# Attention and routed experts on one core: the first routing round's comparisons, counts and pick cut in halves and 128 columns wide, fewer warming products, and a new order of the experts' work

## The chip, the cores and the metric

The kernel runs on one core of a Trainium2 chip. The metric is the device time of one execution, in microseconds (us); lower is better. TensorE (PE) has two clock levels, 1.2 and 2.4 GHz; the profile lists the granted clock as a share of the higher one. PE does the matrix products, VectorE (DVE) and ScalarE (ACT) the elementwise work, GpSimd (POOL) issues the gathers and scatters of rows by index, SyncE (SP) issues the other transfers.

## The reference

Windowed attention with four sink positions makes a table `x` of 3072 tokens by 512. A gate gives each token a logit for each of 8 experts. The pairs of token and expert are taken in falling order of logit; a token goes to the first expert that still has room (384 places). Each expert runs a two-layer network on its 384 tokens.

```python
logits = x @ w_gate
order = np.argsort(-logits.flatten())
for idx in order:
    tok, e = idx // E, idx % E
    if assigned[tok] >= 0 or counts[e] >= cap: continue
    assigned[tok] = e; counts[e] += 1
for e in range(E):
    mask = assigned == e
    out[mask] = np.maximum(x[mask] @ w1[e], 0.0) @ w2[e]
```

## The kernel before

**Attention** (the first 152 us) works on 24 blocks of 128 tokens and writes `x` to memory and the logits to `L`. Its order is not touched.

**Routing** runs in 8 rounds, one for each expert that fills up (`phase`, L534). A round finds the logit at which the first expert is full by a search over the bits of the logits in six steps (`STEPS`: two steps of 64 candidates, four of 32). One step is a chain between two engines: DVE compares all 24 columns of tokens with the candidates (`compare`, L486, writes `cmp`), PE counts per expert (L557, the comparison is the weight operand, the experts' mask `oh` streams), DVE finds the step's digit (`i`, L574 or L580 to 585), PE spreads it over the partitions (L589 or L590, the "digit product" below), DVE forms the next threshold (`xb`) and compares again. At the end of a round come ranks (L617, L618), a comparison of ranks (`lo` against a row of 64) and a second product, the pick (L636), whose result are the indices `idx` of the expert's tokens. In the first round the counts are 24 products whose weights are 64 or 32 columns wide, and the pick is 24 products of 64 columns; in later rounds several columns are packed to 128, so 12 or 6 products do.

**An expert** (`rows`, `weights`, `mlp`): POOL gathers the token rows into `xg0`, `xg1`, `xg2` (L682); PE turns them (L689) into `pt`, `py0`, `py1`; ACT makes the high part `xh` (L700), DVE the low part `xl` (L702). Weights come in 8 loads of 512 KB into four buffers `raw0` to `raw3` (L673); ACT makes the high part `wh` (L675), DVE the low part `wl` (L677). For the first expert, loads 2 to 7 wait until `xg2` has landed (L663, "rowed"). A tile of the first layer is `ph` (eight tiles, f = 0 to 7); for each of four chunks c it takes three products: `xh` with `wh`, `xh` with `wl`, `xl` with `wh` (L722), 96 products per expert. ACT applies Relu (`hh`), DVE makes the low part `hl`. The second layer sums into `py` (L734, 72 products), ACT copies it to `yo`, POOL scatters it to the output (L739).

**Order.** Every engine runs its own list in order. `Graph.order` makes these lists for the routing and the experts: a list scheduler with estimated costs and delays, in which each task's priority is its longest path to the end plus a number for its class (`BIAS`: R for the routing of a round, X for turning, M for products and so on). `run` (L755) also puts warming products (128x384, results unused, L532) in gaps of PE's list between the first pick and the first expert's products, as many as its estimate of the gap holds (L762). In the first round `WARM` gives each step one or two warming products ahead of its counts, and three ahead of the pick.

## Time and profile before

| | |
|---|---|
| median of 3 runs | 502.12 us (499.77 to 504.07) |
| the profiled execution's own time | 499.03 us |
| its span in the trace | 497.3 us |
| busy share of the span: PE, DVE, ACT, POOL | 95%, 77%, 47%, 30% |
| mean granted clock of PE | 0.976 |

The profiled execution is one run, so rows of its trace add up to 499.03 us: 497.3 us of span and 1.7 us around it. A busy share counts a product from its start to its modelled end, and products overlap; so the spacing of products (time of a chain divided by their number) says more than the mean length of one. Positions below are us from the start of the span.

### The profile page before, as it was taken

The numbers are of one execution on the slowest core, as the hardware profiler recorded it, in microseconds if no ns is written. First come the engines' busy times: TensorE is split into PE (matmuls) and PEld (weight loads), VectorE is DVE, ScalarE is ACT, GpSimd is POOL, SyncE is SP. The second block draws the span as 40 slices with busy tenths as digits, with TensorE's granted clock in tenths as the row PEclk, the third lists the DMA queues.
The fourth block names the chain that finished last, engine by engine and source line by source line (L and its number), as shares of the span: only waits on it lengthen the run. The fifth ranks groups of instructions, "written<-read, shape, count | busy, mean of one in ns | idle before, by whom it ended". The sixth has DMA issues, their size and how long they took to land. (4 is left out here: it accounts for less than half of the span.)

```text
span 497.3 us, 11371 instructions
## 1 busy us (share of the span) xinstructions
PE 470.7 (95%) x4167; PEld 388.5 (78%) x4167; DVE 380.9 (77%) x1141; ACT 233.7 (47%) x672; POOL 148.3 (30%) x210
## 2 busy tenths in 40 slices
PE   8999999999997698999999999998999999999994
PEld 4878788887875466878878978876887888988983
DVE  5699989999997589989898898897899864640200
ACT  4678887787860045344353362353352265531210
POOL 6567575665541020030222110032201251001001
PEclk9999999999997589999999999999999999999998
DMA  8556677766412264472572470571652787401001
GB/s 267 190 168 177 176 193 198 207 174 173 106 46 65 68 201 138 153 198 89 177 238 79 165 244 37 164 233 71 209 156 80 229 265 245 173 0 43 21 22 43
DMA packets 75464, 73.13 MB, mean 147 GB/s; under 512 B 28560, under 2 KB 57872, under 8 KB 75408
## 3 DMA queue, kind: packets, MB, share of 16 engines
q1 hardware_dynamic: 70992, 59.29, 40.3%
q0 software_dynamic: 3840, 12.59, 7.4%
q8 instruction: 33, 0.54, 0.4%
q10 hardware_dynamic: 576, 0.52, 0.4%
q14 instruction: 23, 0.19, 0.1%
HBM read 59.80 MB, written 12.58 MB: 146 GB/s over the span
## 5 line engine op out<-in xcount | busy, mean ns | idle before, releaser
L675 ACT ACTIVATE wh<-raw 128x1024 fp32r<-128x1024 f32 x64 | 67.7, 1061 | 76.9 <-DMA raw<-w 41.4
L722 PE MATMUL ph<-xh,wh 128*128 128x384 f32 x256 | 91.4, 357 | 1.0 <-DVE hl L726 0.7
L677 DVE TENSOR_TENSOR wl<-raw,wh 128x1024 fp32r<-128x1024 f32 x64 | 77.5, 1216 | 18.6 <-ACT wh L675 18.3
L722 PE MATMUL ph<-xl,wh 128*128 128x384 f32 x256 | 86.5, 338 | 0.4 <-DVE xl L712 0.4
L722 PE MATMUL ph<-xh,wl 128*128 128x384 f32 x256 | 86.2, 337 | 0.0
L739 POOL DMA_INDIRECT out<-yo,idx x24 | 26.1, 1088 | 178.3 <-ACT yo L737 132.0
L734 PE MATMUL py<-wh,hh 128*128 128x512 f32 x192 | 78.3, 408 | 0.5 <-ACT yo L737 0.4
L734 PE MATMUL py<-wh,hl 128*128 128x512 f32 x192 | 75.5, 393 | 0.3 <-DVE hl L726 0.2
L734 PE MATMUL py<-wl,hh 128*128 128x512 f32 x192 | 75.3, 392 | 0.0
L96 ACT ACTIVATE P<-pp,nmx 128x132 f32<-128x132 f32 x192 | 68.6, 370 | 8.0 <-DVE nmx L91 6.6
L725 ACT ACTIVATE hh<-ph 128x384 fp32r<-128x384 f32 x64 | 31.1, 487 | 78.4 <-PE ph L722 63.4
L81 PE MATMUL pp<-kk,q 64*128 64x260 f32 (+1 forms) x384 | 60.7, 421 | 2.3 <-ACT P L96 1.0
L726 DVE SCALAR_TENSOR_TENSOR hl<-ph,hh 128x384 fp32r<-128x384 f32 x64 | 34.6, 550 | 31.4 <-ACT hh L725 31.1
L682 POOL DMA_INDIRECT xg<-x_dram,idx x24 | 27.6, 1150 | 102.0 <-PE ph L722 41.4
L722 PEld LDWEIGHTS ph<-xh,wh 128*128 128x128 f32 x256 | 48.2, 188 | 4.7 <-DVE hl L726 2.4
L722 PEld LDWEIGHTS ph<-xh,wl 128*128 128x128 f32 x256 | 48.2, 188 | 1.3
L722 PEld LDWEIGHTS ph<-xl,wh 128*128 128x128 f32 x256 | 48.0, 188 | 1.2 <-DVE xl L712 0.7
L81 PEld LDWEIGHTS pp<-kk,q 64*128 64x128 f32 x384 | 33.7, 208 | 14.4 <-ACT P L96 7.3
L734 PEld LDWEIGHTS py<-wh,hl 128*128 128x128 f32 x192 | 36.0, 188 | 9.1 <-DVE hl L726 1.2
L734 PEld LDWEIGHTS py<-wh,hh 128*128 128x128 f32 x192 | 36.2, 188 | 8.0 <-issue 2.0
L91 DVE TENSOR_REDUCE nmx<-pp 128x2 f32<-128x264 f32 x96 | 39.8, 426 | 1.0
L103 ACT ACTIVATE PT<-pp 128x512 f32<-128x512 f32 x48 | 28.7, 597 | 24.0 <-PE pp L102 19.7
(172 smaller groups left out, 827.7 us busy)
## 6 DMA issues: line engine op xcount, KB each, us to landing
raw<-w SPq DMA_DIRECT2D x64, 512.0 KB, 4.7
v<-vd SPq DMA_DIRECT2D x24, 256.0 KB, 3.6
x_dram<-xt SPq DMA_DIRECT2D x24, 256.0 KB, 3.1
kk<-kd SPq DMA_DIRECT2D x23, 264.0 KB, 4.4
q<-qd SPq DMA_DIRECT2D x22, 256.0 KB, 4.3
xg<-x_dram,idx POOLq DMA_INDIRECT x24, 4.1
out<-yo,idx POOLq DMA_INDIRECT x24, 3.0
us<-ud SPq DMA_DIRECT2D x1, 274.5 KB, 5.7
```

The source lines that it names most:

```text
L81: PE.matmul(sp[:,s,:n],q[p,g,:],kk[p,g,k0:k0+n],start=True,stop=True)
L91: V.tensor_reduce(T('nmx',c)[:,2*g:2*g+2],sp[:,:,o:o+132],AX.X,OP.max,negate=True)
L96: A.activation(T('P',c)[:,4*s+g,:],sp[:,s,o:o+132],AF.Exp,bias=T('nmx',c)[:,h:h+1],scale=1.0,accum_out=T('sm',c)[:,h:h+1])
L103: def op_pe(c,g): A.activation(T('PT',c)[:,4*g:4*g+4,:].rearrange("p j (s n)->p s j n",s=2),T('p',c,f'T{g}')[:,:,0:256].rearrange("p s (j ...
L675: g.add('A',947,lambda wh=wh,raw=raw: nc.scalar.activation(wh,raw,AF.Copy),[f'raw{n%4}'],[f'wh{s}'],f'H{k}.{j}',f'W{k}')
L677: g.add(e,{'V':1135,'P':2303}[e],lambda wh=wh,wl=wl,raw=raw,e=e: (nc.vector if e=='V' else nc.gpsimd).tensor_tensor(wl,raw,wh.bitcast(F32) ...
L682: g.add('P',1450,lambda t=t: nc.gpsimd.indirect_dma_start(out=self.xg[t],out_offset=None,in_=self.x_dram,in_offset=bass.IndirectOffsetOnAx ...
L722: nc.tensor.matmul(p[:,0:CAP],x[:,c,:],y[:,c,:],start=c==0 and i==0,stop=c==3 and i==2)
L725: g.add('A',371,lambda f=f,p=p: nc.scalar.activation(self.hh[:,f,:],p[:,0:CAP],AF.Relu),ps,[f'hh{f}'],f'hh{k}.{f}',f'H{k}')
L726: g.add('V',469,lambda f=f,p=p: nc.vector.scalar_tensor_tensor(self.hl[:,f,:],p[:,0:CAP],0.0,self.hh[:,f,:].bitcast(F32),op0=OP.max,op1=OP ...
L734: nc.tensor.matmul(p,x[:,f,ts],w,start=f==0 and i==0,stop=f==7 and i==2)
L739: st=nc.gpsimd.indirect_dma_start(out=self.out,out_offset=bass.IndirectOffsetOnAxis(ap=idx[:,t:t+1],axis=0),in_=y,in_offset=None)
```

## The change

1. **Halves (first round only).** From the second step on, the comparison is issued as two: 13 of 24 columns, then 11 (64 candidates); 15, then 9 (32 candidates). The counts are issued as two tasks of 12 products, of which the first needs only the first comparison. The comparison of ranks and the pick are cut the same way, and the small operations `hi`, `R`, `R3` on which the pick also rests go ahead of the comparison.
2. **128 columns.** The counts and the pick of the first round read 128 columns of the comparison as weights for each product, where they read 64 or 32; the rows that belong to the next columns are not used. `cmp` gets 64 spare columns, zeroed by two more POOL memsets at the start of the program.
3. **Low parts last.** For the first two tiles of the first expert the four chunks' `xh` products come first, the four `xl` products last (8 tasks instead of 4).
4. **Turning first.** The second round's first counts are held until the first expert's rows are turned.
5. **Fewer warming products** after the first pick: a gap holds (gap - 400)/260 instead of (gap - 170)/165.
6. **Order searched anew:** all of `BIAS` is new, and a table `TW` gives single tasks a number of their own.

```diff
-        pri=[-(rank[i]+bias.get(T[i][5],0.0)) for i in range(n)]
+        pri=[TW.get(i,0)-(rank[i]+bias.get(T[i][5],0.0)) for i in range(n)]
...
-        self.cmp=[t([128,64*NC],BF,f"cmp{j}") for j in range(2)]
+        self.cmp=[t([128,64*NC+64],BF,f"cmp{j}") for j in range(2)]
...
+        for x in self.cmp: g.memset(x[:,64*NC:],0.0)
...
+                if n and first:
+                    hv=NC//2+128//m-1
+                    v(u(hv*m/2),lambda j=j,m=m,hv=hv: self.compare(j,xb[j],m,0,hv),f'xb{j}',cn+'a')
+                    v(u((NC-hv)*m/2),lambda j=j,m=m,hv=hv: self.compare(j,xb[j],m,hv,NC),f'xb{j}',cn)
...
-                    for c in range(h):
-                        nc.tensor.matmul(cnt[0:z*m,0:z*E],self.cmp[j][:,c*z*m:c*z*m+z*m],self.oh[:,z*c:z*c+z],start=c==0 and (end or not first),stop=c==h-1)
+                    for c in range(c0,c1):
+                        nc.tensor.matmul(cnt[:,0:z*E],self.cmp[j][:,c*z*m:c*z*m+128],self.oh[:,z*c:z*c+z],start=c==0 and (end or not first),stop=c==h-1)
...
+        if first:
+            hv=NC//2+1
+            v(u(hv*32),lambda: self.compare(oj,self.lo,64,0,hv,OP.is_equal,F16),'lo R3',on+'a')
+            v(u((NC-hv)*32),lambda: self.compare(oj,self.lo,64,hv,NC,OP.is_equal,F16),'lo',on)
...
+            for c in range(c0,c1): nc.tensor.matmul(ip[:,0:6*zp],OH[:,64*zp*c:64*zp*c+128],self.R3[:,:,zp*c:zp*c+zp].rearrange("p g j -> p j g"),start=c==0,stop=c==h-1)
...
-                    g.add('E',125,lambda t=t,d=d,tp=tp: turn(t,d,tp),[f'xg{t}'],ts,f'X{k}.{d}.{t}',f'X{k}')
+                    g.add('E',125,lambda t=t,d=d,tp=tp: turn(t,d,tp),[f'xg{t}'],ts+['turned'],f'X{k}.{d}.{t}',f'X{k}')
...
+            three=((wh,self.xh[b],'h'),(wl,self.xh[b],'h'),(wh,self.xl[b],'l'))
+            parts=[[(c,i) for i in range(3)] for c in range(4)] if k or f>1 else [[(c,0),(c,1)] for c in range(4)]+[[(c,2)] for c in range(4)]
...
-            if s-te>340 and te>=tr: ex.append((te+1,int((s-te-170)//165)))
+            if s-te>340 and te>=tr: ex.append((te+1,int((s-te-400)//260)))
```

On DVE, after the ranks of the first round (`q` holds ranks, `lo` and `hi` their low and high bits, `cmp0` the comparison, `R3` what the pick streams). Before:

```order
L623 TENSOR_TENSOR si_104<-q_131 128x24
L625 TENSOR_SCALAR lo_109<-si_104 128x48
L489 TENSOR_TENSOR cmp0_114<-lo_109,row_66 128x1536
L624 TENSOR_SCALAR hi_132<-si_104 128x24
L630 TENSOR_TENSOR R_150<-hi_132,g6_133 128x144
L632 TENSOR_TENSOR R3_151<-R_150,tid_88 128x144
```

Now:

```order
L631 TENSOR_TENSOR si_104<-q_131 128x24
L632 TENSOR_SCALAR hi_132<-si_104 128x24
L633 TENSOR_SCALAR lo_109<-si_104 128x48
L638 TENSOR_TENSOR R_152<-hi_132,g6_133 128x144
L639 TENSOR_TENSOR R3_153<-R_152,tid_88 128x144
L490 TENSOR_TENSOR cmp0_114<-lo_109,row_66 128x832
L490 TENSOR_TENSOR cmp0_114<-lo_109,row_66 128x704
```

The three small operations moved from behind the comparison to its front, and the comparison is two.

On PE, from the turning of the first expert's last rows to its first products. Before, with ten warming products and the second round's second counts (12 products) in between:

```order
L689 MATMUL pt_2436<-idt_62,xg2_2426 128x64 x4
L689 MATMUL py0_2439<-idt_62,xg2_2426 128x64
...
L532 MATMUL ph1_2438<-onesb_80 128x384
...
L557 MATMUL pr0_2441<-oh_111,cmp1_115 128x16
...
L722 MATMUL ph0_2437<-xh0_2427,wh0_2400 128x384
L722 MATMUL ph0_2437<-xh0_2427,wl0_2412 128x384
L722 MATMUL ph0_2437<-xl0_2429,wh0_2400 128x384
```

Now, with the second round's first counts (12 products) in between:

```order
L704 MATMUL pt_2438<-idt_62,xg2_2428 128x64 x4
L704 MATMUL py0_2441<-idt_62,xg2_2428 128x64
...
L562 MATMUL pr0_2443<-oh_111,cmp0_114 128x16
...
L738 MATMUL ph1_2440<-xh0_2429,wh0_2402 128x384
L738 MATMUL ph1_2440<-xh0_2429,wl0_2414 128x384
L738 MATMUL ph0_2439<-xh0_2429,wh0_2402 128x384
```

No warming product stands there now, and the first `xl` product comes after 14 products with `xh`. Ahead of it, from the first pick on, there were 23, 5 and 3 warming products around the turns of `xg0`, `xg1`, `xg2`; there are 19 ahead of `xg0`, none ahead of `xg1` and 2 ahead of `xg2`, and the second round's first counts moved behind the turns.

On DVE, the work on the first expert's weights beside the second round's steps (`odd`, `two`, `i81` find the digit, `P0` and `xb` form the threshold). Before:

```order
L677 TENSOR_TENSOR wl1_2413<-raw1_2397,wh1_2401 128x1024
L580 TENSOR_SCALAR odd_120<-pr0_2441 64x16
L581 TENSOR_TENSOR two_121<-pr0_2441,odd_120 64x16
L584 TENSOR_SCALAR odd_120<-two_121 32x8
L585 SCALAR_TENSOR_TENSOR i81_117<-two_121,odd_120 32x8
L677 TENSOR_TENSOR wl2_2414<-raw2_2398,wh2_2402 128x1024
L597 TENSOR_REDUCE P0_123<-pr1_2442 128x1
L600 TENSOR_TENSOR xb1_108<-x0_105,P0_123 128x48
L489 TENSOR_TENSOR cmp1_115<-xb1_108,row_66 128x768
```

Now:

```order
L515 CAST df_113<-di_112 128x120
L692 TENSOR_TENSOR wl1_2415<-raw1_2399,wh1_2403 128x1024
L692 TENSOR_TENSOR wl0_2414<-raw0_2398,wh0_2402 128x1024
...
L593 SCALAR_TENSOR_TENSOR i80_116<-pr0_2443,odd_120 64x8
L692 TENSOR_TENSOR wl2_2416<-raw2_2400,wh2_2404 128x1024
L605 TENSOR_REDUCE P1_124<-pr1_2444 128x1
L608 TENSOR_TENSOR xb0_107<-x1_106,P1_124 128x48
L575 SCALAR_TENSOR_TENSOR x0_105<-P1_124,y_103 128x24
L490 TENSOR_TENSOR cmp0_114<-xb0_107,row_66 128x768
```

`wl1` moved ahead of all of the second round's steps (it stood in the third), and `wl2` moved from the step before the fourth counts (`cmp1`) to the step before the third (`cmp0`). Behind that `cmp0` the two `hl` of the first two tiles follow, as one does in the list of before.

## Rows read from the trace of the kernel before

**Rows 1.** Waits of PE from 183 us on: total, times, longest (first and last of 7).
```profile
PE pr L590 <- DVE i L585: 2.0, 2, 1.8
...
PE py L734 <- DVE hl L726: 0.2, 1, 0.2
```

**Rows 2.** Chain that ended last, in order of time: start, us, what.
```profile
422.29 4.19 PE ph L722 x24
...
488.08 2.72 DMA out<-yo,idx
```

**Rows 3.** Two-us stretches: length, busy us of the engines, PE clock, DMA share, GB/s.
```profile
154.00:156.00 2.00, 0.97 (x26) 0.98 (x25) 1.76 (x17) 0.00 (x0) 0.00 (x0) 1.00 0.93 208
156.00:158.00 2.00, 1.18 (x16) 0.78 (x16) 1.44 (x4) 0.00 (x0) 1.40 (x6) 0.60 0.00 0
...
176.00:178.00 2.00, 2.00 (x11) 1.12 (x10) 1.97 (x10) 0.50 (x1) 1.53 (x2) 0.78 0.63 207
...
190.00:192.00 2.00, 0.55 (x7) 0.45 (x8) 1.83 (x9) 0.20 (x1) 0.00 (x0) 1.00 0.72 264
```

**Rows 4.** Timeline of PE, first round to first expert: start, us, what, idle before.
```profile
157.37 1.44 PE L557 MATMUL pr<-oh,cmp 128*64 128x8 bf16 x24 [0.82 <-DVE cmp L489]
...
162.24 0.80 PE L557 MATMUL pr<-oh,cmp 128*32 128x8 bf16 x24 [0.43 <-DVE cmp L489]
...
171.52 1.40 PE L636 MATMUL pr<-R,cmp 128*64 128x6 f16 x24 [1.39 <-DVE R L632]
172.85 5.88 PE L532 MATMUL ph<-onesb 128*128 128x384 bf16 x23
...
181.25 0.34 PE L689 MATMUL pt<-idt,xg 64*128 64x64 f32 x4
...
181.68 1.80 PE L532 MATMUL ph<-onesb 128*128 128x384 bf16 x10
...
183.62 0.42 PE L722 MATMUL ph<-xh,wh 128*128 128x384 f32 x1
```

**Rows 5.** Timeline of DVE, the same stretch.
```profile
156.36 0.96 DVE L489 TENSOR_TENSOR cmp<-xb,row 128x1536 bf16<-128x1536 bf16 x1
...
161.62 0.56 DVE L489 TENSOR_TENSOR cmp<-xb,row 128x768 bf16<-128x768 bf16 x1
...
169.89 0.96 DVE L489 TENSOR_TENSOR cmp<-lo,row 128x1536 f16<-128x1536 int16 x1
...
188.80 1.22 DVE L677 TENSOR_TENSOR wl<-raw,wh 128x1024 fp32r<-128x1024 f32 x1
```

**Rows 6.** Weight loads of 153 to 185 us by shape: busy us, mean ns.
```profile
L532 PEld LDWEIGHTS <-onesb 128*128 128x128 bf16 x52 | 5.3, 112 | 6.1 <-issue 4.5
L557 PEld LDWEIGHTS <-cmp 128*32 128x32 bf16 x96 | 2.9, 103 | 2.2 <-DVE cmp L489 2.2
...
L636 PEld LDWEIGHTS <-cmp 128*64 128x64 f16 x24 | 1.4, 154 | 2.0 <-DVE cmp L489 1.5 <-issue 0.5
```

**Rows 7.** The tile `xg`, 165 to 200 us: time from issue to landing.
```profile
DMA to landing us min/median/max: 3.5/3.5/4.0
```

**Rows 8.** Timelines of POOL, SP and ACT: last gather, a weight load, two activations.
```profile
176.31 1.53 POOL L682 DMA_INDIRECT xg<-x_dram,idx  x1 [0.30 <-issue]
...
180.72 0.37 SPq L673 DMA_DIRECT2D raw<-w  x1
...
181.63 0.38 ACT L700 ACTIVATE xh<-pt 128x256 fp32r<-128x256 f32 x1 [0.27 <-PE pt L689]
...
185.59 1.06 ACT L675 ACTIVATE wh<-raw 128x1024 fp32r<-128x1024 f32 x1 [3.23 <-DMA raw<-w]
```

**Rows 9.** Timeline of PE, 184 to 200 us: the 25th product of the first expert.
```profile
191.76 0.45 PE L722 MATMUL ph<-xh,wh 128*128 128x384 f32 x1 [0.46 <-DVE hl L726]
```

**Rows 10.** Timelines at the two ends of the program.
```profile
5.28 0.43 DVE L88 COPY_PREDICATED pp<-m,big 128x256 f32<-128x256 int32 x1 [1.05 <-POOL big L49]
...
491.56 0.97 POOL L739 DMA_INDIRECT out<-yo,idx  x1 [2.52 <-ACT yo L737]
```

More of the change, by code (lines that the diff above doesn't have):

```diff
@@ L718, in mlp, with mm @@
             wh,wl=[a[s].rearrange("p (d f) -> p d f",d=4)[:,:,128*(f%2):128*(f%2)+128] for a in (self.wh,self.wl)]
-            for c in range(4):
-                def mm(c=c,p=p,wh=wh,wl=wl):
-                    for i,(x,y) in enumerate(((wh,self.xh[b]),(wl,self.xh[b]),(wh,self.xl[b]))):
-                        nc.tensor.matmul(p[:,0:CAP],x[:,c,:],y[:,c,:],start=c==0 and i==0,stop=c==3 and i==2)
-                g.add('E',528,mm,[f'wh{s}',f'wl{s}']+([f'xh{b}.{c}',f'xl{b}.{c}'] if k else [f'{x}{b}.{c}.{t}{j}' for x in ('xh','xl') for t in range(3) for j in range(1+c//2)])+([pn if c==1 else pn+f'.{c-1}'] if c else []),[pn] if c==0 else [pn+f'.{c}'],f'M{k}.{f}.{c}',cls)
-            ps=[pn]+[pn+f'.{c}' for c in (1,2,3)]
+            three=((wh,self.xh[b],'h'),(wl,self.xh[b],'h'),(wh,self.xl[b],'l'))
+            parts=[[(c,i) for i in range(3)] for c in range(4)] if k or f>1 else [[(c,0),(c,1)] for c in range(4)]+[[(c,2)] for c in range(4)]
+            for n,part in enumerate(parts):
+                def mm(part=part,three=three,p=p,last=n==len(parts)-1,n=n):
+                    for c,i in part: nc.tensor.matmul(p[:,0:CAP],three[i][0][:,c,:],three[i][1][:,c,:],start=n==0 and i==0,stop=last and i==2)
+                c=part[0][0]; need=sorted({'x'+three[i][2] for c,i in part})
+                g.add('E',176*len(part),mm,[f'wh{s}',f'wl{s}']+([f'{x}{b}.{c}' for x in need] if k else [f'{x}{b}.{c}.{t}{j}' for x in need for t in range(3) for j in range(1+c//2)])+([pn if n==1 else pn+f'.{n-1}'] if n else []),[pn] if n==0 else [pn+f'.{n}'],f'M{k}.{f}.{n}',cls)
+            ps=[pn]+[pn+f'.{n}' for n in range(1,len(parts))]
             g.add('A',371,lambda f=f,p=p: nc.scalar.activation(self.hh[:,f,:],p[:,0:CAP],AF.Relu),ps,[f'hh{f}'],f'hh{k}.{f}',f'H{k}')
@@ L771 @@
 WARM=[2, 2, 2, 1, 1, 1, 3]
[L772 to L773 removed]
+WIN=[219, 3569667, 2736]
```

29 lines of the change are left out of this document (17 added, 12 removed).

## The prediction

> **What bounds the kernel now.** I read the busy shares first (the table above): PE works 95% of the span, no other engine over 77%. The waits of PE say where that leaves room: from 183 us on, where the experts' products run, seven kinds of wait sum to 5.8 us [rows 1]. So behind 183 us PE is the bound; a better order can win at most about 6 us there, and an earlier first product moves the end by as much, as long as PE isn't starved later. The chain that ended last confirms it for the second half: it is nearly all products, 24 in 4.19 us, 0.175 us each, and at the end a scatter's landing [rows 2]. The room is ahead of that: between 152 and 183 us PE is fed by a chain of small steps. In the two-us stretches [rows 3] PE is busy half of 154 to 156 us, the clock falls to its lower level at 156.4 us (0.60 is the mean of 156 to 158) and is back at 176.9 (0.78), after 4 us of warming products that began at 172.85 [rows 4]. So the change has to be read from the chain that starts at the second step of the first round and ends at the first expert's product at 183.62 us, and then from what follows it. All times below are on the clock of the profiled execution (499.03 us).
>
> **Halves and wide loads in the counts.** From comparison to first count 1.01 us pass for 1536 elements (156.36 to 157.37) and 0.62 for 768 (161.62 to 162.24) [rows 4, 5]: 0.51 ns per element and 0.23 fixed. A first half of 832 elements releases PE after 0.65 us, the second half of 704 after some 0.46 more (0.36 and an estimated 0.1 to issue). The counts' spacing is the weight load's: 24 of 64 columns in 1.44 us, less the last one's own 0.19, are 0.054 each; 24 of 32 columns in 0.80, less 0.17, are 0.027 [rows 4]. For 128 columns at the low clock no count exists. The bounds: as fast as 32 columns, 0.027, or by columns four times that, 0.107. I take 0.027, since a 128-column load of the same type lasts 112 ns on average in this stretch, beside 103 for 32 columns and 154 for 64 [rows 6].
> - Second step: before, the last count starts at 157.37+23x0.054 = 158.61. Now the second twelve start at 156.36+1.11 = 157.47 (the first twelve end before), the last at 157.47+11x0.027 = 157.77. Gain 0.84 us.
> - Third to sixth step: the first half has 480 elements and releases PE after 0.47, 0.15 earlier; the second is done before PE has counted twelve (0.32). Gain 0.15 in three, about 0.1 in the third step, where two warming products stand ahead: 0.55.
> - First step: nothing; its last columns come late as before. One more count waits for them (0.03).
>
> Sum 1.4 us. With loads at 0.107 the last count of a step would start 2.46 us after its first, against 1.24 and 0.61 now.
>
> **Pick.** Before, it starts 1.63 us after its comparison (169.89 to 171.52); 1.01 is the comparison, 0.62 are `hi`, `R`, `R3`. Of these about 0.4 now go ahead (`hi` fits beside `lo`). The first half ends and releases at 169.89+0.4+0.65 = 170.94, the second at 171.40, and the last of the pick starts at 171.40+0.3 = 171.70, against 171.52+23x0.053 = 172.74. Gain 1.0. So `idx` and the gathers come 2.4 us earlier.
>
> **From gather to first product.** The last gather is issued at 176.31 and lands 4.0 later (the longest of three) [rows 7, 8]: 180.3. Now 177.9. But PE turned it only at 181.25, because warming products and the second round's counts stood ahead. Now 19 warming products follow the pick. At the low clock one takes 0.32 (384 columns at 1.2 GHz), at the high one 0.16; 23 took 5.88. From 171.9, with the clock back after 4 us again, 19 end at about 177.0, the first two turns (0.7) at 177.7, the two warming products at 178.0: PE is ready as the rows land. Turn at 178.0. If the clock stays low the 19 alone end at 178.0 and the turn comes at about 179.3; that is the other bound. Behind the turn ten warming products took 1.80 [rows 4]; they are gone. ACT starts its high parts 0.38 after the turn and takes 0.38 [rows 4, 8]; with a release of 0.2 the first product starts at 178.0+0.96 = 179.0, just as the twelve counts are through. Before: 183.62. Gain 4.65, of which 2.4 come from the first round and the rest from what no longer stands in PE's list. The low parts last mean that the 14 products with `xh` need no DVE work on rows; that hides the `xl` (DVE makes them during these 14x0.175 = 2.5 us).
>
> **What is late next.** The second round. In the new list its third counts come after 24 products, and they need a comparison queued on DVE behind `wl2`, which needs load 2, which waits for the last gather. A load issued at 180.72 was in ACT's hands at 185.59, and ACT takes 1.06 [rows 8]. Issue now at 177.9+0.4 = 178.3; `wh2` done at 178.3+4.87+1.06 = 184.2; `wl2` starts at 184.35. PE has then long finished its 24 products and two counts (179.0+4.2+0.9 = 184.1) and waits some 2.5 us, since the next products are queued behind these counts. Before, there was the same wait: from `wl` at 188.80 [rows 5] to the 25th product at 191.76 [rows 9] it took 2.96 us. 184.35+2.96 = 187.3. So the 25th product comes 4.45 us earlier, not less, since `wl1` is no longer between. After it I walked the lists to the 49th product (`wl5`, `wl4` at 1.14 each on DVE, steps of about 1 us between): PE waits once more, about 0.2 us, and stands 4.5 us ahead. The second round's steps are one behind the old list there, but reach their ranks earlier in time.
>
> **The two ends.** The two new memsets stand ahead of `big`, and DVE's first masking waits 1.05 us for it [rows 10]: nothing hides them. POOL's small memsets here follow one another closely, so 0.1 us lost, between 0 and 0.3. At the end, the former scatter lands at 490.8 [rows 2], and the last is issued only at 491.56 [rows 10]; the chain puts the former before it. In the new list 24 products, not 15, follow the last product of the tile before, so that scatter is through by then: 0 to 0.7 gained, I take 0.3.
>
> **The middle.** Between 192 us and the end, the order is all new. Counting rows between a digit product and the next counts, in both lists PE has three to six products of 0.175 or 0.23 there and DVE one `wl` or two smaller parts, a threshold and a comparison; neither list is looser in sum. The gathers of later rounds get as much cover or slightly less. I take 0, from -3.4 (all later waits gone: 5.8 less the 2.4 at 190) to +3.
>
> **Sum:** 4.5 - 0.1 + 0.3 + 0 = 4.7; I keep 4.5, as the estimated clock is the good case. 499.03 - 4.5 = 494.5 on the profiled execution, which was 3.1 us under the median shown; on that median 502.12 - 4.5 = **497.6 us**.
>
> A rule weighed against it. In the group of loads above, 128 columns of a 2-byte type last like 32 [rows 6]. The Trainium skill ("TensorE: Matmul & The Clock Gate", section "LDWEIGHTS (loading the stationary operand)") says a load takes its column count over 1.2 GHz, so 107 ns; its section on the fast weight load on the same page says that full 128-column weights that are not FP32 load about twice as fast as that, measured. By the first rule the sum turns into a loss, by the second nearly into nothing; the row speaks for neither price, which is why both are a rival with a small chance.
>
> **The rivals.**
> 1. *The wide loads cost their columns.* The place is the five counts and the pick of the first round. At 0.107 the last count comes 0.86 later than before in the second step, 1.7 in each of the next four and 0.7 in the pick: 8.4 lost instead of 2.4 won, 502.1-4.5+10.8 = 508.4. At 0.054 it is 501.1. It decides against the change from about 0.07. Against it: rows 6. Chance 0.05.
> 2. *DVE sets the pace of the later rounds* (the other side). In rounds 2 to 6 there are 60 half steps, each a wait if DVE's rows are longer than PE's. 0.075 us more in each takes back the 4.5, 0.16 more makes it slower by 1%. At 0.1: 503.6. For it: the new list puts a `wl` or its like into nearly every half step. Against: the waits of before were 3.4 us for all of these [rows 1]. Chance 0.07.
> 3. *The early gain is eaten:* load 2 lands later, or the clock falls in the wait at 184 to 187 us and the products run at half rate for about 4 us (2 lost), or is late at 176. At 190 to 192 us PE was busy 0.55 of 2.00 us and the clock stayed [rows 3]. 500 to 502. Chance 0.20.
> 4. *The new order also removes later waits:* 494 to 496. Chance 0.16.
>
> My forecast has 0.52, with a range of its own from 495 to 500.
>
> **How the numbers follow.** Range: from case 4 to the upper end of case 3, 493 to 502.5; about 0.1 lies above (rivals 1, 2 in most part) and 0.07 below. About 1%, or 5 us, is what a measurement of this kernel tells from no change. Faster than 497.1: 0.42 (0.24 of the forecast, 0.16 of case 4, 0.02 of case 3). Slower than 507.1: 0.06 (0.03 each of rivals 1 and 2). Within: 0.52.
>
> **What would show it.** Counts of the second step at 0.027 us spacing and the first pick some 2.4 us nearer to its round's start; the first product 4 to 5 us nearer to the end of attention; one PE wait of 2 to 3 us behind the 24th product, released by a comparison behind `wl2`; PE's waits behind that of 2 to 5 us. Wrong it would be by counts at 0.054 or more, a clock that is low behind the first product, or a sum of later waits well over 5 us.

## The result, and the profile after

The changed kernel takes **496.56 us** (median of 4, 495.84 to 497.00), the kernel before 501.91 beside it (499.77 to 504.07): a ratio of 0.989, with an interval of 0.985 to 0.994. Later, beside other executions of the kernel before, the changed kernel gave 497.25 us (0.983, 0.974 to 0.991) and 495.39 us (0.985, 0.980 to 0.990). The ratios leave out slow executions, those more than 1.5% above the fastest of the same kernel, and the medians do not; for 497.25 us that leaves two of six, so that ratio counts for little. So the change makes the kernel faster by 1 to 2%.

The profiled execution of the changed kernel took 497.00 us, with a span of 495.3 us. Attention's length differs by several us between executions of the same attention code (the last section). So places are compared from the end of attention: the first warming product of the routing, at 153.39 us before and here at

```profile
154.76 0.48 PE L533 MATMUL pr<-onesb 128*128 128x384 bf16 x2 [0.85 <-DVE xt L142]
```

All places written with a + below are us from that row. The column "predicted" is the prediction's places less 153.39; its last two rows are the places of before less the sum's 4.5 and 4.7 us.

| place | before | after | predicted |
|---|---|---|---|
| `idx` of the first round | +19.57 | +17.01 | +17.2 |
| first product of the first expert | +30.24 | +25.33 | +25.6 |
| 25th product | +38.38 | +33.51 | +33.9 |
| last instruction of PE | +336.47 | +333.14 | +332.0 |
| end of the span | +343.94 | +340.54 | +339.2 |

The 2.03 us between the two profiled executions are: attention 1.37 later, the way to the 25th product 4.87 shorter, from there to PE's last instruction 1.54 longer, the rest 0.07 shorter.

**The first round.** Timelines of PE (start, us, what, idle before and its releaser), from one digit product to the next. Before:

```profile
155.92 0.16 PE L589 MATMUL pr<-i,wt 128*128 128x1 bf16 x1 [0.41 <-DVE i L574]
159.07 0.16 PE L589 MATMUL pr<-i,wt 128*128 128x1 bf16 x1 [0.26 <-DVE i L574]
161.18 0.16 PE L589 MATMUL pr<-i,wt 128*128 128x1 bf16 x1 [0.25 <-DVE i L574]
...
168.68 0.20 PE L617 MATMUL pr<-M,ltf 128*128 128x48 bf16 x1 [1.01 <-DVE M L610]
```

After:

```profile
157.29 0.16 PE L597 MATMUL pr<-i,wt 128*128 128x1 bf16 x1 [0.42 <-DVE i L582]
...
158.38 0.92 PE L562 MATMUL pr<-oh,cmp 128*128 128x8 bf16 x24 [0.25 <-DVE cmp L490]
159.56 0.16 PE L597 MATMUL pr<-i,wt 128*128 128x1 bf16 x1 [0.26 <-DVE i L582]
...
160.46 0.80 PE L562 MATMUL pr<-oh,cmp 128*128 128x8 bf16 x24
161.51 0.16 PE L597 MATMUL pr<-i,wt 128*128 128x1 bf16 x1 [0.25 <-DVE i L582]
...
168.56 0.20 PE L625 MATMUL pr<-M,ltf 128*128 128x48 bf16 x1 [1.00 <-DVE M L618]
...
170.82 0.92 PE L648 MATMUL pr<-R,cmp 128*128 128x6 f16 x24 [0.81 <-DVE cmp L490]
```

The second step went from 3.15 to 2.27 us, the third from 2.11 to 1.95. The 24 counts of 128 columns take 0.80 us, as the 24 of 32 columns did [rows 4].

**The wait in the second round.** Rows of PE around the second round's third counts (L562, 128x32):

```profile
180.09 0.42 PE L738 MATMUL ph<-xh,wh 128*128 128x384 f32 x1
...
184.87 0.60 PE L738 MATMUL ph<-xl,wh 128*128 128x384 f32 x2
187.71 0.34 PE L562 MATMUL pr<-oh,cmp 128*128 128x32 bf16 x6 [2.25 <-DVE cmp L490]
188.27 0.69 PE L738 MATMUL ph<-xh,wh 128*128 128x384 f32 x1 [0.22 <-DVE hl L743]
188.75 0.52 PE L738 MATMUL ph<-xh,wl 128*128 128x384 f32 x1
189.07 0.52 PE L738 MATMUL ph<-xl,wh 128*128 128x384 f32 x1
```

And the `wh2` and `wl2` that come ahead of it on ACT and DVE, and the comparison itself:

```profile
184.42 1.06 ACT L690 ACTIVATE wh<-raw 128x1024 fp32r<-128x1024 f32 x1 [3.84 <-DMA raw<-w]
...
185.51 1.23 DVE L692 TENSOR_TENSOR wl<-raw,wh 128x1024 fp32r<-128x1024 f32 x1 [0.98 <-ACT wh L690]
...
187.09 0.56 DVE L490 TENSOR_TENSOR cmp<-xb,row 128x768 bf16<-128x768 bf16 x1
```

The first product is the row at 180.09, the 25th that at 188.27. Between the 24th and the counts PE stands still, since the comparison is queued behind `wl2`. Behind the wait the products are 0.32 us apart and more, not 0.175: the clock has gone down. The two-us stretches say the same (length, busy us of PE, PEld, DVE, ACT, POOL, then PE's clock):

```profile
184.00:186.00 2.00, 1.46 (x7) 0.79 (x6) 0.95 (x4) 1.14 (x2) 0.00 (x0) 1.00 1.02 387
186.00:188.00 2.00, 0.29 (x6) 0.24 (x6) 1.97 (x7) 2.00 (x4) 0.00 (x0) 0.79 0.26 95
188.00:190.00 2.00, 1.78 (x7) 1.73 (x6) 1.87 (x7) 1.64 (x2) 0.00 (x0) 0.50 0.76 251
...
194.00:196.00 2.00, 2.00 (x17) 1.76 (x16) 0.78 (x5) 0.27 (x1) 0.00 (x0) 1.00 0.00 0
```

From 187.1 to 194.0 us the clock was at its lower level, 1.2 GHz. Nothing like it stands in the trace of before, where it stayed up from 176.9 to 494.3 us, behind PE's last product; other executions of before did have less clock than that one (the part on the prediction).

The 4.87 us by which the 25th product comes earlier fall into three parts. `wh2` starts 2.54 us earlier (+29.66 against +32.20, the row at 185.59 in [rows 8]). `wl2` follows its start after 1.09 us instead of 3.21, since `wl1` and a digit's operations no longer stand between; before, `wl1` was this row of DVE:

```profile
186.87 1.21 DVE L677 TENSOR_TENSOR wl<-raw,wh 128x1024 fp32r<-128x1024 f32 x1
```

That is 2.12 us, and from `wl2` to the 25th product it takes 0.2 less.

**The waits behind it.** Waits of PE from 183 us on (us in total, times, longest), to be read beside [rows 1]:

```profile
PE pt L704 <- DMA xg<-x_dram,idx: 3.1, 3, 1.6
PE pr L562 <- DVE cmp L490: 2.4, 2, 2.2
PE ph L738 <- DVE hl L743: 0.7, 3, 0.3
PE ph L738 <- DVE xl L727: 0.2, 1, 0.2
```

They sum to 6.4 us, where the kernel before had 5.8. The waits on digits (`i`) and on `yo` are gone; in their place the later experts' turns wait for their gathers, which they did not before. In the two further traces of the changed kernel (next section) these waits for gathers are 4.5 and 3.9 us, and all waits sum to 7.2 and 7.1.

### The profile page after: what moved, and what is told of

It is laid out like the page before. It is cut to its first block, busy times and chain, and to the rows that moved or that the text cites. A ratio compares the mean times of both kernels' runs of the same rounds, so it can differ in the third digit from the quotient of the medians.

```text
span 495.3 us, 11327 instructions
## 1 busy us (share of the span) xinstructions
PE 468.7 (95%) x4147; PEld 386.4 (78%) x4147; DVE 379.8 (77%) x1147; ACT 234.0 (47%) x672; POOL 148.4 (30%) x212
## 4 chain that ended last, share of the span: by engine, by line
PE 61%; DVE 22%; DMA 8%; issue 4%; POOL 2%; ACT 1%; POOLq 0%; SPq 0%; DVEq 0%; ACTq 0%
PE ph L738 20%; PE py L751 15%; PE pp L81 8%; PE pp L122 6%; DVE wl L692 4%; PE pp L140 3%; DMA xg<-x_dram,idx 3%; DVE cmp L490 2%; DMA raw<-w 2%; PE pp L102 2%; DVE hl L743 2%; PE pr L562 2%; DMA out<-yo,idx 1%; DMA kk<-kd 1%; PE pt L704 1%
## 5 line engine op out<-in xcount | busy, mean ns | idle before, releaser
L756 POOL DMA_INDIRECT out<-yo,idx x24 | 24.9, 1038 | 153.6 <-ACT yo L754 119.5
L697 POOL DMA_INDIRECT xg<-x_dram,idx x24 | 29.0, 1209 | 123.1 <-DVE mx L505 34.2
L81 PEld LDWEIGHTS pp<-kk,q 64*128 64x128 f32 x384 | 33.9, 207 | 14.8 <-ACT P L96 7.5
```

The source lines that it names most:

```text
L81: PE.matmul(sp[:,s,:n],q[p,g,:],kk[p,g,k0:k0+n],start=True,stop=True)
L697: g.add('P',1450,lambda t=t: nc.gpsimd.indirect_dma_start(out=self.xg[t],out_offset=None,in_=self.x_dram,in_offset=bass.IndirectOffsetOnAx ...
```

## The experiments

One table holds what the traces gave. "Clock low" is where, behind the first round, the clock was at its lower level (places from the start of the span, the falls ahead of the last 15 us); the last column takes half of that time off the last instruction of PE, as products at the low clock are 0.32 us apart, not 0.175; it is an estimate, and for the first trace of the changed kernel some 0.3 us too much, as PE waits in 0.6 us of its low stretch.

| kernel | attention's end | `idx` | first product | 25th | PE's last | clock low | PE's last, less half of it |
|---|---|---|---|---|---|---|---|
| before | 153.39 | +19.57 | +30.24 | +38.38 | +336.47 | none | 336.5 |
| after | 154.76 | +17.01 | +25.33 | +33.51 | +333.14 | 187.1-194.0 | 329.7 |
| e1_after_again | 154.78 | +17.03 | +26.12 | +33.24 | +334.13 | 255.4-258.8 | 332.4 |
| e9_after_third | 155.43 | +17.03 | +25.59 | +33.72 | +333.32 | 190.5-193.9 | 331.6 |
| e2_narrow | 149.78 | +18.05 | +26.57 | +34.58 | +333.52 | 185.0-188.5 | 331.8 |
| e3_whole | 151.00 | +18.12 | +27.23 | +35.68 | +333.63 | 178.6-182.0 | 331.9 |
| e4_fillwait | 153.10 | +17.03 | +25.63 | +33.31 | +330.10 | none | 330.1 |
| e10_fillwait_again | 155.14 | +17.04 | +26.13 | +34.95 | +333.59 | 181.0-184.4, 256.1-259.5 | 330.2 |
| e5_oldorder | 152.26 | +17.27 | +25.61 | +33.47 | +342.96 | 185.0-191.8, 311.3-314.7, 410.2-413.7 | 336.1 |
| e6_lowplace | 152.52 | +17.01 | +25.76 | +33.36 | +334.47 | 253.0-256.4 | 332.8 |
| e7_oldfill | 153.95 | +17.02 | +26.48 | +33.39 | +331.43 | 187.3-190.8 | 329.7 |
| e8_fillstart | 154.02 | +17.03 | +25.65 | +33.47 | +330.66 | none | 330.7 |
| e12_fillus | 153.69 | +17.03 | +25.75 | +33.41 | +331.57 | 252.4-255.8 | 329.9 |

The kernel without the turning first (e11_noturned) is told below; its waits lie in the low stretches, so the last column has no sense for it.

### The changed kernel again

> The changed kernel, unaltered, as the base of this call. Theory: PE's clock falls in its wait for the second round's third counts (185.1 to 187.7 us in the profile of after) and stays low for 6.8 us, and attention ended 1.4 us later in that profile by a late transfer that is chance. Expected: 496.6 us; attention's end back at 151.5 to 152.0 us (151.5 plus 0.14 for the two memsets) if the late transfer was chance, at 152.9 again if it belongs to the change; the clock low again behind the 24th product if the wait causes it.

> The changed kernel once more, beside the next one on the same chip, since the two profiles of it fell at different places in the clock. Theory (a wait of about 1.7 us or more lets the clock fall in some executions, and a fall costs half of its length): the wait ahead of the second round's third counts is 2.0 to 2.7 us long again, ahead of the third expert's second turn 1.6 to 1.9 us; the clock falls behind one of them or both, and the last PE instruction lies at +333 to +335 from the end of attention; median 496 to 498 us. Rival: the fall was chance of two executions; no fall, last PE at +330 to +331 as with the filled wait.

Measured: 497.25 us (489.14 to 498.26) and 495.39 us (492.67 to 498.27; 496 was the least expected). The 25th product came out within 0.5 us in the three traces. Where the clock falls did not: at the wait ahead of the third counts in two of three, behind the third expert's turn in one. But that wait was not the same either: 2.25 and 2.19 us of idle time where the clock fell, and 1.19 in e1, where it did not:

```profile
187.46 0.32 PE L562 MATMUL pr<-oh,cmp 128*128 128x32 bf16 x6 [1.19 <-DVE cmp L490]
```

In e1 attention ended where it did in the first trace (+1.39 us against before), not back at its earlier place as the expectation's first outcome had it; by its words the delay then belongs to the change. The variants with the same attention code, which ended it between 149.45 and 155.14, say that it varies. Two-us stretches of e1, at the third expert's turn:

```profile
252.00:254.00 2.00, 0.33 (x10) 0.24 (x8) 1.76 (x4) 1.06 (x1) 0.00 (x0) 1.00 0.86 301
254.00:256.00 2.00, 2.00 (x15) 1.49 (x12) 0.74 (x4) 1.73 (x3) 0.00 (x0) 0.84 0.40 93
256.00:258.00 2.00, 2.00 (x6) 1.52 (x6) 1.31 (x4) 0.18 (x1) 0.00 (x0) 0.50 0.52 196
```

PE is busy for 0.33 of 2 us while it waits 1.67 us for a gather, and two us later the clock is down. In the profile of the changed kernel nearly the same wait, 1.56 us at 255.84, had no fall behind it, and neither had the kernel before behind its waits of 1.90 us (at 190.99) and 1.78 (at 340.66). So a wait of this size makes a fall possible, not certain.

### The first round's two edits, each undone

The width (`narrow` undoes the 128 columns and keeps the halves):

```diff
-nc.tensor.matmul(cnt[:,0:z*E],self.cmp[j][:,c*z*m:c*z*m+128],self.oh[:,z*c:z*c+z],...)
+nc.tensor.matmul(cnt[0:z*m,0:z*E],self.cmp[j][:,c*z*m:c*z*m+z*m],self.oh[:,z*c:z*c+z],...)
-nc.tensor.matmul(ip[:,0:6*zp],OH[:,64*zp*c:64*zp*c+128],...)
+nc.tensor.matmul(ip[0:64*zp,0:6*zp],OH[:,64*zp*c:64*zp*c+64*zp],...)
```

> Undoes the 128 columns alone: the first round's counts and pick read 64 or 32 columns as weights again; the halves and the order stay. Theory (a 128-column load costs as much as a 32-column one, 0.027 us at the low clock): second step 0.48 us and pick 0.48 us longer, steps 3 to 6 unchanged; the first product 1.0 us later after the end of attention, 497.5 us in all. Rival (the halves alone carry the gain, the loads hide under the second comparison): within 0.2 us of the base, 496.6.

The halves (`whole` compares all columns in the first half's instruction and leaves the second one empty):

```diff
-self.compare(j,xb[j],m,0,hv)
+self.compare(j,xb[j],m,0,NC)
-self.compare(j,xb[j],m,hv,NC)
+None
```

> Undoes the halves alone: the first round's comparisons and the comparison ahead of the pick are one instruction again, in the order of the changed kernel; the loads stay 128 columns wide. Theory: second step 0.2 us longer, steps 3 to 6 0.15 each, pick 0.2: 0.95 us in all, 497.5. Rival (an instruction more on DVE costs what the earlier start gains): within 0.2 us of the base.

Measured: 496.23 us (0.992, 0.988 to 0.995) and 496.85 us (0.989, 0.985 to 0.993). The medians can't tell either from the changed kernel; the traces can, since `idx` is a short way from attention's end. It lies at +18.05 and +18.12, against +17.01 to +17.03: the width is worth 1.0 us, the halves 1.1. The rest of the 2.56 us by which `idx` is earlier, about 0.45, fits `hi`, `R` and `R3` ahead of the comparison; no run undoes that alone. The second step's counts of `narrow`, and one of its steps with 32 candidates:

```profile
153.40 1.44 PE L562 MATMUL pr<-oh,cmp 128*64 128x8 bf16 x24
156.00 0.80 PE L562 MATMUL pr<-oh,cmp 128*32 128x8 bf16 x24
```

So at the low clock 64 columns are the slow shape: 24 products take 1.44 us, with 32 or 128 columns 0.80. Why, no run here shows. The weight loads of the changed kernel, 153 to 185 us (busy us, mean ns of one, idle before):

```profile
L562 PEld LDWEIGHTS <-cmp 128*128 128x128 bf16 x168 | 5.2, 102 | 4.6 <-DVE cmp L490 4.5
```

One lasts 102 ns on the mean, but products with such loads start 0.027 us apart: the loads overlap. The Trainium skill ("TensorE: Matmul & The Clock Gate", section "LDWEIGHTS (loading the stationary operand)") has a load last its columns over 1.2 GHz, 107 ns for 128. The trace has 102 for these, but 103 for 32 columns and 154 for 64 [rows 6], so a recorded load does not follow its columns. As an estimate by the same rule, 32 and 64 columns take 27 and 53 ns, which is the spacing measured for them (27 and 54); 128 take 107, and there the measured 27 decides against it.

### The wait filled

14 warming products are put in PE's list ahead of the second round's third counts; nothing else moves.

```diff
+        w=next(s for s,i,f in o if g.t[i][4]=='R1.cnt2' and g.t[i][0]=='E')
-        ev=sorted([(s,1,i) for s,i,f in o]+[(s,0,n) for s,n in ex])
+        ev=sorted([(s,1,i) for s,i,f in o]+[(s,0,n) for s,n in ex]+[(w-.001,-1,14)])
...
-            if a==0: self.warm(self.ph[1],i); continue
+            if a<=0: self.warm(self.ph[1] if a==0 else self.pt[1],i); continue
```

> The changed kernel with 14 warming products (128x384, results unused) in PE's list just ahead of the second round's third counts, where PE waits 2.6 us. Theory (the wait makes the clock fall, and the low clock costs 18 products 0.145 us each): the clock stays at its higher level behind the 24th product and the time falls by up to 2.6 us, to 494.0 to 495.0. Rival 1 (PE runs into the next wait earlier: the gathers of rounds 1 to 3 and DVE's steps set the pace): the clock stays up, but 496.0 to 496.6. Rival 2 (the clock falls for another reason): low as before and 496.6.

> The kernel with 14 warming products in the wait ahead of the second round's third counts once more, against the changed kernel on the same chip. Theory: no fall of the clock behind the first product, 25th product at +33.2 to +33.5 from the end of attention, last PE at +330 to +331, 2.5 to 4 us ahead of the changed kernel; median 492.5 to 495 us. Rival: the 493.7 us were chance, the last PE lies within 1.5 us of the changed kernel's.

Measured: 493.67 us (0.985, 0.982 to 0.988) and 494.06 us (0.984, 0.979 to 0.988). PE in e4, at the place of the wait:

```profile
183.96 2.45 PE L533 MATMUL pt<-onesb 128*128 128x384 bf16 x14
186.25 0.30 PE L562 MATMUL pr<-oh,cmp 128*128 128x32 bf16 x6
186.42 0.45 PE L738 MATMUL ph<-xh,wh 128*128 128x384 f32 x1
186.70 0.34 PE L738 MATMUL ph<-xh,wl 128*128 128x384 f32 x1
```

The counts start 0.2 us later than in the changed kernel (+33.15 against +32.95), the 25th product does not (+33.31); the products behind are 0.175 us apart, and PE's last instruction comes 3 to 4 us earlier than in the three traces of the changed kernel. But e10 had it at +333.59, as its rival said: there the clock fell at 181.0, before the first product and behind waits of only 0.66 and 0.53 us, and again behind the third expert's turn, and its expectation that no fall would come is wrong. Over all traces: of eight with this wait unfilled (after, e1, e9, e2, e3, e5, e6, e7) five fell within 2 us of its end; of four with it filled (e4, e8, e10, e12) none did. The eight waits differ: those of 1.99, 2.07, 2.19 and 2.25 us all had a fall, of those of 0.63, 1.19, 1.23 and 1.24 only the last (e3's fall came earlier, at 178.6). With so few traces, that the filling prevents the fall at this place is likely and not shown. Falls at other places it does not prevent. The medians of this version are 1.3 to 3.6 us under those of the changed kernel measured beside it, but the intervals against the kernel before overlap, so that this version is faster than the changed kernel is likely and not shown by the times.

### The old order with the new code

`BIAS` and the scheduler's window `WIN` (new in the change as well, which the list of changes does not say) are those of before, `TW` is empty; all other parts of the change stay.

> The changed code (halves, 128 columns, low parts last, turning first, fewer warming products) with the numbers of the old order: BIAS and the window of before, no TW. Times are counted from the end of attention (the first warming product of the routing). Theory: the first round's 2.5 us come from the code alone, so idx lies at +17.0 as in the changed kernel (+19.6 before); behind it the old numbers were found for another graph, and part of what lies behind is lost: the last PE instruction at +335 to +338 (changed kernel +333 to +334, before +336.5), median 498 to 501 us. Rival 1: the new numbers bring nothing, the code all of it: last PE at +333 to +334, median 496 to 497. Rival 2: the old numbers fit the new graph badly, and the sum of PE's waits behind the first product grows by over 5 us: last PE above +339, median above 502.

Measured: 504.24 us (1.002, 0.998 to 1.006), no faster than before. Up to the 25th product nothing is lost (+33.47). All of it goes behind: PE's last instruction comes 9 to 10 us later than in the three traces of the changed kernel. Waits of PE from 183 us on:

```profile
PE pr L598 <- DVE i L593: 2.8, 3, 1.5
PE pt L704 <- DMA xg<-x_dram,idx: 2.3, 2, 1.7
PE pr L562 <- DVE cmp L490: 2.1, 2, 2.0
PE ph L738 <- DVE hl L743: 1.6, 5, 0.4
```

With three more rows, of 0.7, 0.4 and 0.4, they sum to 10.3 us, 3.1 to 3.9 more than in the changed kernel. Three falls of the clock (13.7 us low in all, about 6.8 lost) stand at waits of 1.99 us for `cmp`, 1.52 for `i` and 1.69 for a gather. The waits and 3.4 to 5.1 more of the clock make up 7.3 to 8.3 of the 8.8 to 9.8 us; the rest is open. So the code and its numbers go together: the numbers of before, found for another graph, give back the whole early gain. Rival 2 of the expectation holds in its places and its time; its sum of waits (over 5 us more) does not.

The early gain, for its part, comes from the code: with the old numbers too `wl1` is done before `wh2` is, and `wl2` starts at +30.50 (+30.75 in the changed kernel). The low parts and the warming products, undone one by one below, leave the 25th product where it is as well. Which part of the code moves `wl1` no run shows; the turning first is the one that none could undo cleanly.

### The low parts back in place

```diff
-[[(c,0),(c,1)] for c in range(4)]+[[(c,2)] for c in range(4)]
+[x for c in range(4) for x in ([(c,0),(c,1)],[(c,2)])]
```

> Of the change, only the low parts last are undone: for the first two tiles each chunk's xl product stands right behind its two xh products, as before the change (still 8 tasks, all other numbers kept). Theory: PE waits for DVE's xl behind the first two xh products, up to 1.5 us in the first eight products, but the second round's third counts, which wait for a comparison behind wl2, take up this wait: the 25th product stays within 0.4 us of the changed kernel's +33.2 to +33.5 from the end of attention, and the end within 1 us (last PE +333 to +334). Rival: the low parts last are worth their wait, so the 25th product comes 1 to 2 us later and the end as well, 498 us.

Measured: 498.45 us (0.994, 0.990 to 0.997). PE behind the first products:

```profile
180.09 0.44 PE L738 MATMUL ph<-xl,wh 128*128 128x384 f32 x1 [0.70 <-DVE xl L717]
...
182.38 0.44 PE L738 MATMUL ph<-xl,wh 128*128 128x384 f32 x1 [0.15 <-DVE xl L717]
...
185.32 0.32 PE L562 MATMUL pr<-oh,cmp 128*128 128x32 bf16 x6 [0.63 <-DVE cmp L490]
```

PE waits 0.85 us for `xl` in two places, and the wait ahead of the third counts is 0.63 us (1.19 to 2.25 in the three traces of the changed kernel); the 25th product stays at +33.36. So the low parts last hide a wait that another one would have taken up. The end is 0.3 to 1.3 us later than in those traces and the median lies where the rival had it, 498; but the rival's cause, a later 25th product, is not there, and whether the end is this edit is open.

### The old number of warming products

```diff
-int((s-te-400)//260)
+int((s-te-170)//165)
```

> Of the change, only the smaller number of warming products is undone: 32 instead of 19 ahead of the turn of xg0, 4 instead of 2 ahead of that of xg2. Theory: the turn of xg2 and the first product come about 1.8 us later (first product at +27 to +28 from the end of attention, +25.3 to +26.1 in the changed kernel), but the 25th product does not (+33.2 to +33.5), since it hangs on wl2; PE's wait ahead of the second round's third counts shrinks from 2.6 us to about 1, the end stays or, if the clock then stays up behind it, comes up to 2.5 us earlier (last PE +331 to +334). Rival: the first product decides, as the prediction counted it, and the end comes 1.8 us later (last PE +335 to +336, 498 us or more).

Measured: 495.52 us (0.988, 0.982 to 0.993). The first product comes at +26.48, 0.4 to 1.2 us later (1.8 was expected), the 25th at +33.39, not later. The wait ahead of the third counts is 1.24 us long there, and yet the clock fell behind it:

```profile
186.78 0.32 PE L562 MATMUL pr<-oh,cmp 128*128 128x32 bf16 x6 [1.24 <-DVE cmp L490]
187.34 0.69 PE L738 MATMUL ph<-xh,wh 128*128 128x384 f32 x1 [0.24 <-DVE hl L743]
```

So fewer warming products bring the first product forward by 0.4 to 1.2 us, and no gain at the end shows: PE's last instruction is 1.7 to 2.7 us earlier in this one trace with the old number, and the median lies among those of the changed kernel.

### The turning first, undone

```diff
-ts+['turned']
+ts
-cn+' oh'+(' turned' if k==1 and n==0 else '')
+cn+' oh'
```

> Of the change, only the turning first is undone: the second round's first counts no longer wait for the first expert's rows to be turned. The lists then differ over the whole second round (wl2 stands behind the third comparison again, its first counts ahead of the turn of xg0). Theory: the turn itself does not come sooner by it, since the rows' landing sets it (first product at +25.3 to +26.5); the wait of 2.6 us ahead of the third counts is gone, and the 25th product comes at +30.5 to +32.5 in place of +33.2 to +33.5; the end keeps 0 to 2 us of it (last PE +331 to +334). Rival: the numbers were found for the order with it, new waits of 2 us or more stand in the later rounds, last PE above +335.

Measured: 519.64 us (1.035, 1.030 to 1.041). The expectation fell. The first product comes in time (+25.30), but in the list that results, PE's counts of several steps of the second round stand one behind another ahead of the 25th product, with waits of 1.6 to 2.3 us at most of them:

```profile
179.36 0.31 PE L562 MATMUL pr<-oh,cmp 128*128 128x32 bf16 x6 [0.31 <-DVE cmp L490]
181.94 0.17 PE L598 MATMUL pr<-i,wt 128*128 128x8 bf16 x1 [2.27 <-DVE i L593]
184.11 0.34 PE L562 MATMUL pr<-oh,cmp 128*128 128x32 bf16 x6 [1.99 <-DVE cmp L490]
186.03 0.17 PE L598 MATMUL pr<-i,wt 128*128 128x8 bf16 x1 [1.58 <-DVE i L593]
...
194.74 0.69 PE L738 MATMUL ph<-xh,wh 128*128 128x384 f32 x1 [0.50 <-DVE hl L743]
```

The 25th product (the row at 194.74) is 11.8 us late, and the clock is low from 181.6 to 198.7. This doesn't price the turning first by itself: it shows what these numbers do to a list that lacks one dependency. Its own price stays open.

### Attention's start

One more warming product at 6 us, on top of the filled wait:

```diff
-            for j in range(c[1]): PE.matmul(d,wz[:,0:128],wz,start=True,stop=True)
+            for j in range(c[1]+(not R.setdefault('f',[]))): PE.matmul(d,wz[:,0:128],wz,start=True,stop=True)
+            R['f'].append(1)
```

> The kernel with 14 warming products in PE's wait ahead of the second round's third counts, and one more warming product (128x512, 0.52 us at the low clock) at 6 us, ahead of the second QK. Attention ended at 149.8 to 154.8 us in the five profiles of changed kernels; it was early where the clock first rose at 11 to 12 us and stayed, late where it rose at 23 us. Theory: the wait of 0.4 to 0.7 us at 8 us decides this; with it filled the clock rises at 11 to 12 us in every run, attention ends at 150 to 151 us, and the median is 490 to 492 us with a spread under 3 us (without the extra product 493.7 and 492.4 to 494.8). Rival: something ahead of the program decides it, so the rise still falls at either place, and the median stays at 493 to 495.

Three and four warming products ahead of the narrow products at 11 and 15 us, also on top of the filled wait:

```diff
+        for j in range(3): PE.matmul(t,wz[:,0:128],wz,start=True,stop=True)
         for j in range(HP): PE.matmul(t[:,0:E],us[:,128*j:128*j+128],...)
...
+        for j in range(4): PE.matmul(t,wz[:,0:128],wz,start=True,stop=True)
         for b in range(B): PE.matmul(t[:,E*b:E*b+E],pk[:,b],U,start=True,stop=True)
```

> The kernel with the filled wait, with 3 warming products (128x512) ahead of the eight 8-column products at 11 us (L62) and 4 ahead of those at 15 us (L67), without the extra one at 6 us. In four of the profiles the clock rose at 7 to 12 us, fell at 14 to 15.5, in the stretch of these narrow products, and was back at 21 to 22. Theory: the narrow products are too little for the clock, and with the seven between them it stays up once it has risen; the rise itself stays at 7 to 12 or moves from 23 to about 12 us, attention ends at 149.5 to 152 us, median 490 to 493. The seven cost 1.5 us at the high clock. Rival: the clock goes its way as before, and the seven cost 1.5 to 3 us: attention's end at 153 to 156, median 494 to 497.

Measured: 494.05 us (0.983, 0.978 to 0.989) and 494.16 us (0.983, 0.978 to 0.987), as the filled wait alone. With the one product the clock rose at 12.1, fell at 15.5 and was back at 22.3: the theory, that this makes it rise and stay in every run, falls. With the seven it rose at 13.4 and stayed, as the theory had it, but attention ended at 153.69, inside the rival's range. That the seven products and the late rise took what the clock gave is argued, not shown.

## Why the prediction was right

The median was forecast at 497.6 us and came to 496.56; the sum, 4.5 us, stands against 5.35 between the medians. But the three traces of the changed kernel end only 2.4 to 3.4 us nearer to attention's end than the one of before. Point by point:

- **Counts, 1.4 us.** Right. From one digit product to the next the second step lost 0.88 us (0.84 was worked out), the third to sixth 0.16, 0.15, 0.14 and 0.15 (0.1 and three times 0.15): 1.48. The price on which it hung, 0.027 us for a 128-column load at the low clock, is what the rows show, so rival 1 is out at both of its prices, 0.107 and 0.054. The reason given for it was weak: it rested on recorded lengths of loads, which do not give the spacing (102 ns against 27), and the 154 ns that it set beside them are of the pick's f16 loads; the counts' own of 64 columns last 134.
- **Pick, 1.0 us.** Right: from the ranks' product to `idx` 4.27 us before, 3.21 now.
- **Gather to first product.** Right in sum (4.91 against 4.65), with one step off: the last turn did not wait for its rows but 0.53 us for ACT, which had to clear `pt` (row 179.16 of the trace: idle 0.53 behind `xh` L715). And what the prediction gave to the warming products that are gone mattered only for the first product, not for the end: with more of them (e7) the 25th comes no later.
- **The wait behind `wl2`.** Right: a wait of some 2.5 us behind the 24th product was foreseen, and 2.25 us of idle time were measured (2.19 and 1.19 in the other two traces); the 25th product was to come 4.45 us earlier, with `wl1` out of the way, and came 4.87 earlier (5.14 and 4.66).
- **The clock in that wait.** The forecast took it to stay up, as in the wait at 190 to 192 us before [rows 3], and had its fall as part of rival 3, with 2 us lost. It fell there, in five of eight traces, for 3.4 or 6.8 us, an estimated cost of 1.7 or 3.4. The step that failed is that one row of before was taken for what such a wait does. A clock that is low behind the first product was one of the prediction's own signs of being wrong. On the two profiled executions alone rival 3 even came out in time: 2.03 us gained in place of 4.5, with 2.9 lost to the clock behind the 25th product and attention 1.37 longer. On the medians it did not (500 to 502 forecast).
- **The middle, 0.** Right on the traces, within what they can tell. From the 25th product to PE's last instruction, with half of the low clock taken off: 298.1 us before; 296.8, 299.2 and 297.9 in the three traces of the changed kernel (for the first, 5.7 of its 6.8 us lie behind the 25th product). But it is a 0 between two large numbers: the old numbers on the new graph would have lost all (e5). Rival 2's price was met there, 503.6 forecast and 504.24 measured, and only a new search avoided it; that the numbers agree is chance, as its cause was a few long waits and the clock, not DVE's pace in every half step. That later rounds' gathers would have "as much cover or slightly less" was too mild: PE waits 3.1 to 4.5 us for them where it didn't before.
- **The ends.** The memsets: DVE's first masking starts at 5.38 us in place of 5.28 and waits 1.20 for `big` [rows 10], 0.1 as predicted. The tail: 0.3 was predicted, 0.07 measured (7.40 us behind PE's last instruction against 7.47). The step that failed was to follow the chain from scatter to scatter. Rows of the last two scatters after:

```profile
484.37 0.97 POOL L756 DMA_INDIRECT out<-yo,idx  x1 [2.99 <-DMA out<-yo,idx]
489.53 0.97 POOL L756 DMA_INDIRECT out<-yo,idx  x1 [4.19 <-ACT yo L754]
```

The last one waits for ACT's copy, as it did before [rows 10]; the former scatter's landing had not held it then either.

So the prediction was right by its steps in the first 190 us. Behind, the fall of the clock was not in its sum; that the medians agree all the same is in part luck. It rests on the place of the profiled execution of before, 3 us under its median, which the forecast carried over.

The granted clock of every execution makes a cause likely. The profiled execution of before had a mean of 0.976; the 54 others of it beside the experiments have 0.966 on the mean, and only four of them reach 0.976. That is an estimated 10 us more at the lower level behind the first rise, up to 5 us of time, in the executions that make its median. The 16 executions of the changed kernel have 0.971. So the trace of before, with no fall among the products, was one of its best in clock, and falls of the clock are not new with the change; by these means the changed kernel spends less time at the lower level. How much of the 5 us between the medians is clock is open: where the others of before fell no trace shows, and single times follow the clock only loosely.

## What to carry to other kernels

In a chain of small products, look at the spacing by weight shape and use the shape that is fast, even if most of its columns are thrown away; and cut a comparison so that its consumer starts on the first part. Before such a gain is counted to the end, ask which wait takes it up (here one of 1.2 to 2.3 us took up the low parts and the warming products whole), and whether an idle PE there costs clock behind it. Read a trace's granted clock beside that of other executions before its waits are taken for the kernel's. Numbers that were searched for one graph belong to that graph: put on another, they cost here all that the change was worth.

## What the runs showed that was not expected

**Attention's end varies by 6 us between traces, with the clock's first rise.** Attention's code is the same in all these kernels but for the two memsets and the few products of e8 and e12. The traces list no level of the clock ahead of its first rise, and the profile shows 1.00 there; that it was low is read from the products, as below. Where the clock rose at 10.9 to 11.3 us and stayed (e2, e3, the kernel without turning first), it ended at 149.45 to 151.00; where it rose at 7.2 to 12.1, fell at 14.1 to 15.5 and was back at 20.9 to 22.3 (e4, e5, e6, e8), at 152.26 to 154.02; where it first rose at 23.2 to 24.0 (before, after, e1, e7, e9, e10), at 153.39 to 155.43 (in e9, the latest, it also fell from 149.5 to 152.9). Traces of one and the same kernel lie closer: 0.7 us apart in the three of the changed kernel, 2.0 in the two with the filled wait. The same eight products in the changed kernel and in e2:

```profile
11.49 1.87 PE L62 MATMUL pp<-us 128*128 128x8 f32 x8
```

```profile
11.11 1.06 PE L62 MATMUL pp<-us 128*128 128x8 f32 x8
```

The 6 us are more than the whole change is worth, and of the size of the spread of before (498.3 to 506.2 us), though one trace of it can't show that this is its cause. What decides where the clock rises stayed open; the two attempts at it (e8, e12) did not settle it.

**Short waits can cost clock in the steady part.** In the stretch of the products PE works nearly without a break, and yet the clock fell at waits of 1.24 to 2.25 us, in some executions and not in others (in e10 behind two of 0.66 and 0.53), and stayed low for 3.4 us or twice that, with PE busy nearly in full. A fall of 3.4 us costs an estimated 1.7 us, about as much as the wait itself.
